# The smaller of two scores, from GpSimd to VectorE, inside a top-32 attention kernel

## The chip, the core and the metric

The kernel is one program on one NeuronCore of a Trainium2 chip. The metric is the time of one execution on the device in microseconds (us); lower is better. A core has TensorE (PE in the profile, its weight loads PEld), VectorE (DVE), ScalarE (ACT), GpSimd (POOL) and SyncE (SP, which issues transfers here).

## What is computed

The reference is attention in which each query keeps its 32 largest scores, then a mixture of eight experts, then a feed-forward layer. The change lies in the first part alone:

```python
B, H, S, D = q.shape                      # 4, 8, 576, 64
top_k = 32
scores = scale * np.matmul(q, k.transpose(0, 1, 3, 2))
kth = np.partition(scores, -top_k, axis=-1)[..., -top_k:-top_k + 1]
mask = scores >= kth
scores = np.where(mask, scores, -1000000000.0)
scores = scores - np.max(scores, axis=-1, keepdims=True)
attn = np.exp(scores)
attn = attn / (np.sum(attn, axis=-1, keepdims=True) + 1e-09)
return np.matmul(attn, v).astype(np.float32)
```

Behind it each token goes to one of 8 experts (512 to 1024 to 512) and then through 512 to 2048 to 512.

## The kernel before

**Units and groups.** The 32 heads are taken as 16 pairs (`j`). A pair has 9 units: 8 tiles of 128 queries of one head, and one tile with the last 64 queries of both heads. A unit's scores are 128 rows of 576 columns. Two units form a group `g`; there are 144 units and 72 groups, so two pairs take nine groups. The order of the work on every engine is the order in which the code is written: one loop over `g`, with background steps attached to a group by `at(g, f, ...)`.

**Scores.** For group `g + 4` TensorE multiplies q and k (both split into a high and a low part, `qh`/`ql` and `kh`/`kl`), and ScalarE copies the result to a tile of four units, `s` (L203). The parts of a pair `j` are made ahead of time: `kh` on VectorE (L170), `kl` on GpSimd (L174), `qh` on GpSimd (L178) in the same group as `kl`, `ql` on GpSimd (L182) one group later. By the loop, `kl` and `qh` of pair `j` stand in group `9j // 2 - 6`.

**Top-32 of a group.** `topk(g)` finds the 32nd largest score of each row on VectorE. A row of 576 is folded twice. `big` is the larger of columns x and x + 288; `c` (144 columns) the larger of the two halves of `big`, `lit2` the smaller of them; `lit` (288 columns) is the smaller of the two scores that `big` was made from. The 8 largest of `lit2` and of `lit` go into 16 further columns of `c`, and then four rounds of "8 largest" (L250, L261) with "replace these 8" (L258) between them are done on 160 columns instead of 576. `edge` and `top` are copied by GpSimd (L234) at the head of the next group, for a check at the end that no row needed more than the 8. `nm`, the bias for the exponential, is one small GpSimd instruction (L251) as soon as the first 8 largest are known.

**Who folds when.** `big`, `c` and `lit2` are made on VectorE for four units at once, two groups ahead: in a group with an odd number, right behind the first "8 largest" (L211 to L213). The first two groups have folds of their own. So there are 35 folds of four units and two of two. `lit` is made apart. For most groups GpSimd makes it, since the larger and the smaller of two numbers add up to their sum, bit pattern by bit pattern: as integers, `lit = a + b - big`, in `less` (L223 the sum, one group ahead, at the head of `topk`; L225 the difference, behind `nm`). In groups 0 and 1 and in the four of `DIRECT` (67, 68, 70, 71) VectorE makes it with one minimum over two units (L239).

**Behind it.** ScalarE makes the exponentials `e` (needs `nm`) and the mask `w` (needs the 32nd), TensorE transposes them, ScalarE copies `a`, TensorE multiplies by v, ScalarE copies `xr`; once per pair VectorE makes the reciprocals `r` (L335, L336), and GpSimd the scaled rows `x` (L339) and `xtail` (L344). From about 500 us on GpSimd also sends rows to memory for the experts (L837).

Of the kernel before, what the change touches and what calls it, by code (L numbers as in the profile page):

```python
# [7 lines left out]
F32 = mybir.dt.float32  # L8
F32R = mybir.dt.float32r
BF16 = mybir.dt.bfloat16  # L10
I32 = mybir.dt.int32
AF = mybir.ActivationFunctionType
ALU = mybir.AluOpType
# [3 lines left out]
B, H, S, D = 4, 8, 576, 64  # L17
# [25 lines left out]
AHEAD = 4  # L43
LEAVE = 3
START = (0, 1, 1, 2, 2, 3)
DIRECT = (67, 68, 70, 71)
FIRST = (0, 4, 9, 13)
NT1 = FIRST[B - 1]
SEG = ((0, 512), (512, S))
# [12 lines left out]
class Kernel:  # L62
# [32 lines left out]
    def attention(self, moe):  # L95
        nc, tc = self.nc, self.tc
        with ExitStack() as ctx:
            P = self.P
# [34 lines left out]
            raw, kq, st, xr = {}, {}, {}, {}  # L133
# [71 lines left out]
            def fold(s):  # L205
                h, q = S // 2, S // 4
                n = s.shape[1]
                big = P.wk.tile([128, n, h], F32, name="big", bufs=1)
                c = P.wk.tile([128, n, q + 16], F32, name="c")
                lit2 = P.wk.tile([128, n, q], F32, name="lit2", bufs=1)  # L210
                nc.vector.tensor_tensor(big, s[:, :, 0:h], s[:, :, h:S], op=ALU.max)  # L211
                nc.vector.tensor_tensor(c[:, :, 0:q], big[:, :, 0:q], big[:, :, q:h], op=ALU.max)
                nc.vector.tensor_tensor(lit2, big[:, :, 0:q], big[:, :, q:h], op=ALU.min)  # L213
                return [[t[:, i:i + 2] for t in (c, lit2, big)] for i in range(0, n, 2)]

            folded, lits, moved = {}, {}, []

            def less(g, parts):

                i = st[g].bitcast(I32)  # L220
                if parts[0]:
                    lits[g] = P.wk.tile([128, 2, S // 2], I32, name="lit")
                    nc.gpsimd.tensor_tensor(lits[g], i[:, :, 0:S // 2], i[:, :, S // 2:S], op=ALU.add)  # L223
                if parts[1]:
                    nc.gpsimd.tensor_tensor(lits[g], lits[g], folded[g][2].bitcast(I32), op=ALU.subtract)  # L225

            def topk(g):
                q = S // 4
                two = range(2)
                after_it = 2 <= g + 1 < ng and g + 1 not in DIRECT  # L230
                if after_it:
                    less(g + 1, (True, False))
                while moved:
                    nc.gpsimd.tensor_copy(*moved.pop(0))  # L234
                if g < 2:
                    folded[g], = fold(st[g])
                if g < 2 or g in DIRECT:
                    lits[g] = P.wk.tile([128, 2, S // 2], I32, name="lit")
                    nc.vector.tensor_tensor(lits[g].bitcast(F32), st[g][:, :, 0:S // 2], st[g][:, :, S // 2:S], op=ALU.min)  # L239
                c, lit2, _ = folded.pop(g)  # L240
                lit = lits.pop(g).bitcast(F32)
                m8 = P.wk.tile([128, 2, TOPK // 8, 8], F32, name="m8", bufs=4)
                z = P.wk.tile([128, 2, q + 16], F32, name="z", bufs=1)
                nm = P.wk.tile([128, 2], F32, name="nm", bufs=4)
                for i in two:
                    nc.vector.max(c[:, i, q + 8:q + 16], lit2[:, i])
                for i in two:
                    nc.vector.max(c[:, i, q:q + 8], lit[:, i])
                for i in two:
                    nc.vector.max(m8[:, i, 0], c[:, i])  # L250
                nc.gpsimd.tensor_scalar(nm, m8[:, :, 0, 0], -0.125, None, op0=ALU.mult)  # L251
                if g % 2 and g + 1 < ng:
                    folded[g + 1], folded[g + 2] = fold(four[g // 2 + 1])
                if after_it:
                    less(g + 1, (False, True))
                for r in range(TOPK // 8 - 1):
                    for i in two:
                        nc.vector.match_replace(out=z[:, i], in_to_replace=m8[:, i, r],  # L258
                                                in_values=c[:, i] if r == 0 else z[:, i], imm_value=LOWEST)
                    for i in two:  # L260
                        nc.vector.max(m8[:, i, r + 1], z[:, i])  # L261
                last = m8[:, :, TOPK // 8 - 1, 7:8]
                moved.append((edge[:, 2 * g:2 * g + 2], c[:, :, q + 7::8]))
                moved.append((top[:, 2 * g:2 * g + 2], last[:, :, 0]))
                return [(last[:, i], nm[:, i:i + 1]) for i in two]
# [88 lines left out]
            ng = nu // 2  # L354
# [25 lines left out]
            for j in range(1, len(pairs)):  # L380
                g = 9 * j // 2 - AHEAD - 4
# [109 lines left out]
            for g in range(ng):  # L491
                for f, a in first.pop(g, []):
                    f(*a)
                tk[g] = topk(g)
                if g > 0:
                    ws = masks(g - 1)
# [1171 lines left out]
```

## Time and profile before

| what | us |
|---|---|
| median of 3 runs | 1267.04 (1265.31 to 1267.12) |
| the profiled execution's own time | 1264.6 |
| its span, first to last instruction | 1263.0 |
| busy in the span: TensorE, VectorE, ScalarE, GpSimd | 1141.2, 925.2, 739.1, 676.8 |
| last "8 largest" of the last group ends | about 535 |
| the feed-forward layer, on TensorE, begins | about 833 |

Busy time is the union of an engine's instructions in the profile. It contains waits that happen inside an instruction: a record that is longer than another of the same operation and shape has waited for something after it was issued. A table row of the trace's list in order of time gives the start, the duration and, where an engine sat idle, for how long and what released it; consecutive instructions of an engine may overlap by some 0.08 us.

### The profile page before, as it was taken

The numbers are of one execution on the slowest core, as the hardware profiler recorded it, in microseconds if no ns is written. First come the engines' busy times: TensorE is split into PE (matmuls) and PEld (weight loads), VectorE is DVE, ScalarE is ACT, GpSimd is POOL, SyncE is SP. The second block draws the span as 40 slices with busy tenths as digits, with TensorE's granted clock in tenths as the row PEclk, the third lists the DMA queues.
The fourth block names the chain that finished last, engine by engine and source line by source line (L and its number), as shares of the span: only waits on it lengthen the run. The fifth ranks groups of instructions, "written<-read, shape, count | busy, mean of one in ns | idle before, by whom it ended". The sixth has DMA issues, their size and how long they took to land. (4 is left out here: it accounts for less than half of the span.)

```text
span 1263.0 us, 25811 instructions
## 1 busy us (share of the span) xinstructions
PE 1141.2 (90%) x9220; PEld 972.8 (77%) x9221; DVE 925.2 (73%) x2573; ACT 739.1 (59%) x1328; POOL 676.8 (54%) x724
## 2 busy tenths in 40 slices
PE   8988899889989997787987898988899999999998
PEld 5766677668767776576776797877799999999997
DVE  6999999999999999986999995658722232222222
ACT  4878787789778886734665666643433333333322
POOL 3877787778777775762666552315532322223221
PEclk7999999989988998998989999999999999999999
DMA  4126463102020102356777777733110101000000
GB/s 90 26 89 203 146 212 116 44 11 49 11 49 11 30 11 86 127 177 199 255 240 242 240 253 240 231 122 109 36 42 9 34 17 34 18 25 26 25 1 25
DMA packets 139219, 123.56 MB, mean 98 GB/s; under 512 B 65408, under 2 KB 102272, under 8 KB 139072
## 3 DMA queue, kind: packets, MB, share of 16 engines
q1 hardware_dynamic: 133312, 108.05, 27.8%
q0 software_dynamic: 3392, 11.27, 2.7%
q10 hardware_dynamic: 2368, 2.39, 0.6%
q8 instruction: 78, 1.28, 0.4%
q14 instruction: 69, 0.57, 0.1%
HBM read 87.07 MB, written 34.60 MB: 96 GB/s over the span
## 5 line engine op out<-in xcount | busy, mean ns | idle before, releaser
L1166 POOL TENSOR_TENSOR gl<-g,gh 128x384 fp32r<-128x384 f32 x96 | 98.4, 1025 | 285.2 <-ACT gh L1165 246.7
L297 PE MATMUL tp<-nhuge,w 128*128 128x128 bf16 x720 | 143.4, 233 | 41.4 <-ACT w L286 41.4
L1327 POOL TENSOR_TENSOR w1l<-w1r,w1h 128x512 fp32r<-128x512 f32 x72 | 103.0, 1433 | 131.9 <-ACT w1h L1326 90.9
L295 PE MATMUL tp<-ident,e 128*128 128x128 f32 x720 | 157.6, 306 | 8.0 <-ACT e L281 8.0
L1161 ACT ACTIVATE c<-c,half 128x384 f32<-128x384 f32 x96 | 59.2, 617 | 178.7 <-DVE c L1160 178.6
L1160 DVE TENSOR_SCALAR c<-h 128x384 f32<-128x384 f32 x95 | 52.7, 555 | 145.4 <-PE h L1019 145.4
L295 PEld LDWEIGHTS tp<-ident,e 128*128 128x128 f32 x720 | 109.7, 152 | 38.4 <-ACT e L281 10.7
L1016 PE MATMUL h<-xh,wih 128*128 128x384 f32 x380 | 129.1, 340 | 1.1 <-ACT xh L1010 1.1
L1017 PE MATMUL h<-xh,wil 128*128 128x384 f32 x380 | 128.8, 339 | 0.0
L286 ACT ACTIVATE w<-s,m 128x576 bf16<-128x576 f32 x144 | 103.5, 769 | 36.9 <-DVE m L261 36.9
L281 ACT ACTIVATE e<-s,nm 128x576 f32<-128x576 f32 x144 | 103.4, 767 | 33.4 <-POOL nm L251 33.2
L1163 DVE TENSOR_TENSOR g<-c,h 128x384 f32<-128x384 f32 x95 | 52.6, 554 | 95.0 <-ACT c L1161 95.0
L1027 PE MATMUL y<-woh,gl 128*128 128x512 f32 x288 | 114.9, 399 | 4.7 <-POOL gl L1166 4.7
L297 PEld LDWEIGHTS <-w 128*128 128x128 bf16 x720 | 81.6, 114 | 48.0 <-ACT w L286 47.7
L261 DVE MAX8 m<-z 128x8 f32<-128x160 f32 x432 | 116.6, 309 | 0.0
L1025 PE MATMUL y<-woh,gh 128*128 128x512 f32 x288 | 112.8, 392 | 3.4 <-ACT gh L1165 3.4
L302 ACT ACTIVATE a<-tp 128x640 f32<-128x640 f32 x144 | 101.6, 706 | 22.4 <-PE tp L297 20.4
L1026 PE MATMUL y<-wol,gh 128*128 128x512 f32 x288 | 113.6, 395 | 0.0
L225 POOL TENSOR_TENSOR lit<-lit,big 128x576 int32<-128x576 int32 x66 | 103.0, 1561 | 1.5 <-POOL nm L251 0.4
L1327 DVE TENSOR_TENSOR w2l<-w2r,w2h 128x512 fp32r<-128x512 f32 x86 | 88.1, 1028 | 20.5 <-ACT w2h L1326 19.8
L314 PE MATMUL tp<-v,a 128*64 128x65 f32 x2880 | 102.4, 226 | 0.3 <-ACT a L302 0.2
L223 POOL TENSOR_TENSOR lit<-s 128x576 int32<-128x576 int32 x66 | 101.9, 1545 | 1.1
(309 smaller groups left out, 3254.8 us busy)
## 6 DMA issues: line engine op xcount, KB each, us to landing
w1r<-in_moe_w_dram SPq DMA_DIRECT2D x88, 256.0 KB, 3.7
w2r<-in_moe_w_dram SPq DMA_DIRECT2D x88, 256.0 KB, 3.6
xs_dr<-zero SPq DMA_DIRECT2D x19, 512.0 KB, 4.7
ys_dr<-zero SPq DMA_DIRECT2D x19, 512.0 KB, 5.4
cr<-in_moe_w_in_dram SPq DMA_DIRECT2D x16, 512.0 KB, 4.5
cr<-in_moe_w_out_dram SPq DMA_DIRECT2D x13, 512.0 KB, 3.6
rows<-xs_dr SPq DMA_DIRECT2D x20, 256.0 KB, 2.8
rk<-in_k_dram SPq DMA_DIRECT2D x32, 128.0 KB, 2.6
```

Of the source, the lines that this page charges most:

```text
L225: nc.gpsimd.tensor_tensor(lits[g], lits[g], folded[g][2].bitcast(I32), op=ALU.subtract)
L261: nc.vector.max(m8[:, i, r + 1], z[:, i])
L281: nc.scalar.activation(e, s, AF.Exp, bias=nm, scale=0.125)
L286: nc.scalar.activation(w, s, AF.Relu, bias=t, scale=-1.0)
L295: nc.tensor.matmul(o, e[:, k0:k0 + 128], self.ident, is_transpose=True, start=True, stop=False)
L297: nc.tensor.matmul(o, w[:, k0:k0 + 128], self.nhuge, start=False, stop=True)
L1016: nc.tensor.matmul(p, wh[c], xh[:, c, :], start=c == 0, stop=False)
L1017: nc.tensor.matmul(p, wl[c], xh[:, c, :], start=False, stop=False)
L1025: nc.tensor.matmul(y[t], hh[:, o], wh, start=first, stop=False)
L1026: nc.tensor.matmul(y[t], hh[:, o], wl, start=False, stop=False)
L1027: nc.tensor.matmul(y[t], hl[:, o], wh, start=False, stop=last)
L1327: sub(l, w, h.bitcast(F32), op=ALU.subtract)
```

## The change

The minimum `lit` moves into `fold`, on VectorE, for four units at once and right behind `lit2`. `less`, `DIRECT` and GpSimd's two integer operations per group are gone. The four later groups that VectorE served apart, and the first two, now take `lit` from their fold too.

```diff
-DIRECT = (67, 68, 70, 71)
...
                 lit2 = P.wk.tile([128, n, q], F32, name="lit2", bufs=1)
+                lit = P.wk.tile([128, n, h], F32, name="lit", bufs=1)
                 nc.vector.tensor_tensor(big, s[:, :, 0:h], s[:, :, h:S], op=ALU.max)
                 nc.vector.tensor_tensor(c[:, :, 0:q], big[:, :, 0:q], big[:, :, q:h], op=ALU.max)
                 nc.vector.tensor_tensor(lit2, big[:, :, 0:q], big[:, :, q:h], op=ALU.min)
-                return [[t[:, i:i + 2] for t in (c, lit2, big)] for i in range(0, n, 2)]
-
-            folded, lits, moved = {}, {}, []
-
-            def less(g, parts):
-
-                i = st[g].bitcast(I32)
-                if parts[0]:
-                    lits[g] = P.wk.tile([128, 2, S // 2], I32, name="lit")
-                    nc.gpsimd.tensor_tensor(lits[g], i[:, :, 0:S // 2], i[:, :, S // 2:S], op=ALU.add)
-                if parts[1]:
-                    nc.gpsimd.tensor_tensor(lits[g], lits[g], folded[g][2].bitcast(I32), op=ALU.subtract)
+                nc.vector.tensor_tensor(lit, s[:, :, 0:h], s[:, :, h:S], op=ALU.min)
+                return [[t[:, i:i + 2] for t in (c, lit2, lit)] for i in range(0, n, 2)]
+
+            folded, moved = {}, []
 
             def topk(g):
                 q = S // 4
                 two = range(2)
-                after_it = 2 <= g + 1 < ng and g + 1 not in DIRECT
-                if after_it:
-                    less(g + 1, (True, False))
                 while moved:
                     nc.gpsimd.tensor_copy(*moved.pop(0))
                 if g < 2:
                     folded[g], = fold(st[g])
-                if g < 2 or g in DIRECT:
-                    lits[g] = P.wk.tile([128, 2, S // 2], I32, name="lit")
-                    nc.vector.tensor_tensor(lits[g].bitcast(F32), st[g][:, :, 0:S // 2], st[g][:, :, S // 2:S], op=ALU.min)
-                c, lit2, _ = folded.pop(g)
-                lit = lits.pop(g).bitcast(F32)
+                c, lit2, lit = folded.pop(g)
...
                 if g % 2 and g + 1 < ng:
                     folded[g + 1], folded[g + 2] = fold(four[g // 2 + 1])
-                if after_it:
-                    less(g + 1, (False, True))
```

Line numbers after L213 differ between the two programs: `kl`, `qh`, `ql` are L174, L178, L182 before and L173, L177, L181 after, `nm` is L251 and L236, the copies `edge` and `top` are L234 and L223, the "8 largest" L246, L248, L250, L261 are L231, L233, L235, L244.

GpSimd's queue in groups 3 and 4, before: from the `nm` of group 3 to the `nm` of group 4 and its `ql`.

```order
L251 TENSOR_SCALAR nm<-m_572 128x2
L225 TENSOR_TENSOR lit<-lit,big 128x576
L174 TENSOR_TENSOR kl<-kT,kh 128x576
L178 TENSOR_TENSOR qh_115<-qT,zero 128x512
L223 TENSOR_TENSOR lit<-s 128x576
L234 COPY edge<-c 128x4
L234 COPY top<-m_572 128x2
L251 TENSOR_SCALAR nm<-m_680 128x2
L225 TENSOR_TENSOR lit<-lit,big 128x576
L182 TENSOR_TENSOR ql_116<-qT,qh_115 128x512
```

The same stretch after:

```order
L236 TENSOR_SCALAR nm<-m_566 128x2
L173 TENSOR_TENSOR kl<-kT,kh 128x576
L177 TENSOR_TENSOR qh_115<-qT,zero 128x512
L223 COPY edge<-c 128x4
L223 COPY top<-m_566 128x2
L236 TENSOR_SCALAR nm<-m_673 128x2
L181 TENSOR_TENSOR ql_116<-qT,qh_115 128x512
```

`kl` and `qh` now stand right behind `nm`, as does `ql` one group on.

GpSimd's queue from the `x` of group 16 to the `ql` of group 17, before.

```order
L339 TENSOR_TENSOR x_73<-xr,r 128x4x128
L344 TENSOR_TENSOR xtail_77<-xr,r 64x64 x2
L223 TENSOR_TENSOR lit<-s_1903 128x576
L234 COPY edge<-c 128x4
L234 COPY top<-m_2097 128x2
L251 TENSOR_SCALAR nm<-m_2208 128x2
L225 TENSOR_TENSOR lit<-lit,big 128x576
L182 TENSOR_TENSOR ql_118<-qT,qh_117 128x512
```

The same stretch after:

```order
L322 TENSOR_TENSOR x_73<-xr,r 128x4x128
L327 TENSOR_TENSOR xtail_77<-xr,r 64x64 x2
L223 COPY edge<-c 128x4
L223 COPY top<-m_2066 128x2
L236 TENSOR_SCALAR nm<-m_2174 128x2
L181 TENSOR_TENSOR ql_118<-qT,qh_117 128x512
```

Only the three short instructions are left between `xtail` and `ql`.

VectorE's queue at the fold in group 3, before (`m` is the tile of the 32 largest, `lit_584` is `lit2`).

```order
L250 MAX m_572<-c 128x8 x2
L211 TENSOR_TENSOR big<-s 128x1152
L212 TENSOR_TENSOR c<-big 128x4x144
L213 TENSOR_TENSOR lit_584<-big 128x576
L258 MATCH_REPLACE z<-m_572,c 128x160 x2
```

The same place after (`lit_578` is `lit2`):

```order
L235 MAX m_566<-c 128x8 x2
L211 TENSOR_TENSOR big<-s 128x1152
L212 TENSOR_TENSOR c<-big 128x4x144
L213 TENSOR_TENSOR lit_578<-big 128x576
L214 TENSOR_TENSOR lit<-s 128x1152
L241 MATCH_REPLACE z<-m_566,c 128x160 x2
```

One instruction, the minimum of 1152 columns, has come between `lit2` and the first match.

## Rows read from the trace of the kernel before

**Rows 1.** The page, part 1: busy us (share of the span) and instructions.

```profile
PE 1141.2 (90%) x9220; PEld 972.8 (77%) x9221; DVE 925.2 (73%) x2573; ACT 739.1 (59%) x1328; POOL 676.8 (54%) x724
```

**Rows 2.** Busy us by stretch: length, engines with instructions, granted clock, DMA share, GB/s.

```profile
40.00:535.00 495.00, 432.17 (x5355) 354.62 (x5352) 491.33 (x1861) 395.77 (x696) 379.44 (x464) 0.95 0.25 76
```

**Rows 3.** Groups on GpSimd, 40 to 480 us: count, busy us, mean ns, idle before.

```profile
L225 POOL TENSOR_TENSOR lit<-lit,big 128x576 int32<-128x576 int32 x62 | 96.8, 1562 | 1.4 <-POOL nm L251 0.4
```

**Rows 4.** VectorE in order of time, fold of group 3: start us, duration us.

```profile
43.28 1.33 DVE L211 TENSOR_TENSOR big<-s 128x1152 f32<-128x1152 f32 x1
44.65 0.76 DVE L212 TENSOR_TENSOR c<-big 128x576 f32<-128x576 f32 x1
45.32 1.98 DVE L213 TENSOR_TENSOR lit<-big 128x576 f32<-128x576 f32 x1
47.23 0.08 DVE L258 MATCH_VALUE_LOAD z<-m,c 128x8 f32 x1
```

**Rows 5.** GpSimd in order of time, the same fold.

```profile
43.45 1.24 POOL L251 TENSOR_SCALAR nm<-m 128x2 f32<-128x2 f32 x1 [1.65 <-DVE m L250]
44.76 1.92 POOL L225 TENSOR_TENSOR lit<-lit,big 128x576 int32<-128x576 int32 x1
46.65 1.94 POOL L174 TENSOR_TENSOR kl<-kT,kh 128x576 fp32r<-128x576 f32 x1
```

**Rows 6.** VectorE in order of time, fold of group 69 and around it.

```profile
515.18 0.82 DVE L248 MAX8 c<-lit 128x8 f32<-128x288 f32 x2 [0.55 <-POOL lit L225]
...
516.37 1.34 DVE L211 TENSOR_TENSOR big<-s 128x1152 f32<-128x1152 f32 x1
...
519.09 0.08 DVE L258 MATCH_VALUE_LOAD z<-m,c 128x8 f32 x1
...
522.77 1.60 DVE L239 TENSOR_TENSOR lit<-s 128x576 f32<-128x576 f32 x1
```

**Rows 7.** VectorE in order of time, the fold that group 1 makes for itself.

```profile
23.20 1.54 DVE L212 TENSOR_TENSOR c<-big 128x288 f32<-128x288 f32 x1
24.66 1.51 DVE L213 TENSOR_TENSOR lit<-big 128x288 f32<-128x288 f32 x1
26.10 1.82 DVE L239 TENSOR_TENSOR lit<-s 128x576 f32<-128x576 f32 x1
```

**Rows 8.** GpSimd in order of time, the same fold.

```profile
22.58 1.84 POOL L174 TENSOR_TENSOR kl<-kT,kh 128x576 fp32r<-128x576 f32 x1 [5.00 <-DVE kh L170]
24.39 1.47 POOL L178 TENSOR_TENSOR qh<-qT,zero 128x512 fp32r<-128x512 f32 x1
25.94 1.36 POOL L182 TENSOR_TENSOR ql<-qT,qh 128x512 fp32r<-128x512 f32 x1
```

**Rows 9.** Line L239: duration ns least/median/most, first and last start.

```profile
L239 DVE TENSOR_TENSOR lit<-s x6: 737/752/1820, 14.9 to 529.3; 128x576 f32<-128x576 f32 x6
```

**Rows 10.** GpSimd in order of time, ahead of the fold of group 17.

```profile
141.82 1.88 POOL L344 TENSOR_TENSOR xtail<-xr,r 64x64 f32<-64x64 f32 x2
```

**Rows 11.** VectorE in order of time, fold of group 23.

```profile
182.97 2.00 DVE L211 TENSOR_TENSOR big<-s 128x1152 f32<-128x1152 f32 x1
...
185.69 3.50 DVE L213 TENSOR_TENSOR lit<-big 128x576 f32<-128x576 f32 x1
```

**Rows 12.** GpSimd in order of time, the same fold.

```profile
185.80 1.40 POOL L225 TENSOR_TENSOR lit<-lit,big 128x576 int32<-128x576 int32 x1
187.16 1.41 POOL L223 TENSOR_TENSOR lit<-s 128x576 int32<-128x576 int32 x1
```

**Rows 13.** VectorE in order of time, fold of group 9.

```profile
88.44 0.75 DVE L213 TENSOR_TENSOR lit<-big 128x576 f32<-128x576 f32 x1
```

**Rows 14.** GpSimd in order of time, the same fold.

```profile
88.56 1.91 POOL L225 TENSOR_TENSOR lit<-lit,big 128x576 int32<-128x576 int32 x1
```

**Rows 15.** VectorE in order of time, fold of group 13.

```profile
114.10 1.71 DVE L212 TENSOR_TENSOR c<-big 128x576 f32<-128x576 f32 x1
```

**Rows 16.** Line L335: duration ns least/median/most, first and last start.

```profile
L335 DVE TENSOR_SCALAR r<-xr x20: 96/160/1287, 78.5 to 543.1; 128x9 f32<-128x9 f32 x15, 128x2 f32<-128x2 f32 x4, 128x1 f32<-128x1 f32 x1
```

## The prediction

> **What bounds the kernel now.** I read the page's busy line first: over the whole span no engine but TensorE is above 73% [rows 1]. That average mixes stages, so I took the busy time by stretches next. From 40 to 535 us VectorE works 491.3 of 495 us, TensorE 432, ScalarE 396 and GpSimd 379 [rows 2]. So up to the last top-32 (about 534 us) the time is the length of VectorE's queue, and what a change adds to that queue or takes from it moves everything behind it by as much. GpSimd's part of the job (L225 and its twin L223, two integer operations per group) takes 1.56 us apiece and 96.8 us for the 62 instances of L225 between 40 and 480 us [rows 3]. It is large, but GpSimd is not the bound.
>
> Then I looked inside a fold, because its durations don't fit its sizes. In the fold at 43.28 us, `big` (1152 columns) takes 1.33 us and `c` (576) 0.76, but `lit2`, of the same size as `c`, takes 1.98; from the start of `big` to the first match it is 3.95 us [rows 4]. GpSimd shows why: its L225 was issued 0.11 us into `c`, took 1.92 us, and `lit2` ends only after it; the next GpSimd operation, a `kl`, then lasts 1.94 because `lit2` was in front of it [rows 5]. Two-input operations of the two engines exclude each other, and they alternate. Of the 35 four-unit folds 27 last 3.93 to 4.01 us like this one. At 516.37 us, where GpSimd has no such work, the same three operations need 2.72 us [rows 6] (one other fold, at 502.82, is like it). So GpSimd's two operations are not free to VectorE: they cost it about 1.2 us per fold.
>
> **The change, part by part.** *Added:* one minimum over 1152 columns per four-unit fold, 35 of them. Its nearest row is `big`, of the same shape: 1.33 us, of which some 0.08 overlaps the next instruction (as `lit2` and the match do in [rows 4]), so 1.25. A fold that GpSimd leaves alone becomes 2.72 + 1.25 = 3.97 us. Against today's 3.95 that is nothing: the relief of `lit2` pays for the new operation almost exactly. The result hangs on the folds that are not left alone.
>
> *Moved:* with L223 and L225 gone, GpSimd's remaining two-input work (`kl` and `qh`, then `ql` one group later, for each head pair) moves forward to right behind `nm`, as the rows of order show. `nm` is released just before the fold; so in a group with odd number this work now meets the fold, where before it came later and met the matches, which don't mind. By the loop, `kl`+`qh` come in an odd group for pairs 2, 3, 6, 7, 10, 11, 14, 15 (eight folds) and `ql` for six others. That they alternate with VectorE, one for one, the fold at 22.42 us shows, the only one where GpSimd has a run of such work today: `c` and `lit2`, of 288 columns and so shorter than the 0.76 us of [rows 4], take 1.54 and 1.51, and the 576 columns of `lit` 1.82 where its like take 0.75 (the middle of L239 [rows 9]), each behind one of `kl`, `qh`, `ql` [rows 7, 8]. So:
> - `kl`+`qh` in a fold: `lit2` waits for `kl` (1.21: 1.97 as today behind L225, less 0.76), `lit` for `qh` (1.07: 1.82 less 0.75): 3.97 + 2.28 = 6.25 us, against 3.95 today.
> - `ql` in a fold: 3.97 + 1.07 = 5.05.
> - In six of these fourteen (groups 17, 21, 35, 39, 53, 57) `x` and `xtail` of the group before come first. Today the second `xtail` is caught by `big` there: the pair takes 1.88 us from 141.82, with the `big` of that fold inside [rows 10]. Behind it now stand `edge`, `top` and `nm`, short ones, and then `ql` or `kl`+`qh`. Who goes first then is a race that the trace shows both ways. At 182.97 `lit2` lost to L225 and L223, one after the other, and took 3.50 us [rows 11, 12]; at 88.44, with L225 issued 0.12 us after it instead of 0.11, it took 0.75 and L225 waited [rows 13, 14]. Four folds went the second way, three the first. Won, the short ones cost the fold some 0.2 us: 4.2. Lost, `lit2` waits for them (0.4 us) and for `ql` as well (1.3 [rows 8]): 3.97 + 1.7 = 5.7; with `kl`+`qh`, of which the second comes before `lit2` or before `lit`, 1.25 more: 6.95. These are estimates from those rows.
>
> The sum over the 35 folds. Today: 27 x 3.95, three at 4.91 (a late `qh` makes `c` 1.71 us long [rows 15]), three at 6.15 [rows 11], two at 2.72 or a little more = 145.3 us. After: 21 alone x 3.97 = 83.4; five with `kl`+`qh` x 6.25 = 31.3; three with `ql` x 5.05 = 15.2; the six doubtful ones 25.2 if all are won, 38.0 if all are lost, 31.6 with half of each, which I take, since the trace has four to three. Total 161.5 (155.1 to 167.9), so +16.2 (+9.8 to +22.6).
>
> *Removed from VectorE:* the four separate minima of groups 67, 68, 70, 71 (L239), three at 0.67 (0.75 less the overlap) and the one at 522.77, behind an `x`, at 1.53 [rows 6, 9]: -3.5. The `r` of three groups, which stood up to 1.29 us instead of the middle 0.16 behind a late `qh` [rows 16]: -3.4. The wait of 0.55 us for the last L225, before the max at 515.18 [rows 6]: -0.5. Sum of these -7.4. In groups 0 and 1 the same minimum merely changes its line: nothing.
>
> *Costed at nothing:* GpSimd's lost 200 us, hidden already under a full VectorE; the new tile `lit`, as large as the two it replaces, read and written by VectorE alone; the longer fold's effect on `w` and `e` on ScalarE and on the copies behind it, which are late with VectorE and not in addition to it. What is queued behind a delayed `lit` is the match loop of the group, and with it all that I count. After 535 us no instruction changes, and I let the shift pass through unaltered.
>
> **Net: +16.2 - 7.4 = +8.8 us** (+2.4 to +15.2 from the race alone). The profiled execution took 1264.6 us, so 1273.4; the median of the three runs is 1267.04, which gives 1275.8. I say 1275.
>
> [...] The row to explain is `lit2` at 185.69 us, issued ahead of L225 (185.80) and L223 (187.16) and still behind both [rows 11, 12]. [...]
>
> **The rivals.**
> 1. *VectorE wins all six races.* For it: the four folds like 88.44 us; against: the three like 182.97. Time: +2.4, so 1267.0 by the profiled execution or 1269.4 by the median, at the edge of what can be told from no change. Chance 0.2.
> 2. *The other side: the shared access is simply relieved.* If `kl`, `qh` and `ql` came too late to be queued before `lit2` (`kl` must be issued within 0.63 us of `nm`'s end, which is when `lit2` is), all 35 folds would last 3.97: 139 us, -6.3, with the -7.4 in all -13.7, so 1251 to 1253. It decides when fewer than six of the `kl`+`qh` folds collide, since each costs 2.28. Against it: L225 came 0.07 us after `nm` in [rows 5] and `kl` has nothing else to wait for, its `kh` being ready before the group starts. Chance 0.09.
> 3. *No relief.* If `nm` and the small copies block the fold as L225 does, the new minimum comes on top: 35 x 1.25 - 7.4 = +36, 1301. Against it: in [rows 4, 5] `nm` waits for `big` and ends 0.04 us into `c`, and `c` still takes its 0.76. Chance 0.03.
>
> My own case, with some of the races lost (+5 to +15), has 0.62; 0.06 is left for small mishaps either way.
>
> **How the numbers follow.** This kernel's measurement tells about 0.2% (2.5 us) from no change. Slower by more: my case, rival 3, and the upper half of rival 1: 0.73. Within: the rest of rival 1 and small mishaps: 0.16. Faster: rival 2 and a little: 0.11. The range runs from 1266, just below rival 1, to 1283, all races lost on top of the median; it leaves out rivals 2 and 3.
>
> **What would show it.** Right: the fold's four operations at 1.33, 0.76, 0.76 and 1.33 us in most groups; `lit2` near 1.97 and `lit` near 2.4 in groups 3, 7, 25, 43, 61; `lit2` at 1.8 in 13, 31, 49; `r` never above 0.2 us before 500 us; VectorE still full to about 543 us. Wrong: idle time on VectorE before that, folds of 3.97 in groups 3 and 7 (then rival 2), small copies that hold up `c` (rival 3), or a stretch after 535 us that changes its length.

## The result, and the profile after

The changed kernel took 1278.97 us (median of 4 runs, 1276.64 to 1279.64) against 1267.08 (1265.31 to 1268.04): a ratio of 1.0092, 95% interval 1.0075 to 1.011. A second set on another occasion gave 1276.01 against 1267.34, 1.0069 (1.0045 to 1.0093). So the change made the kernel 9 to 12 us slower. The profiled execution took 1279.38 us.

First the page and the busy time by stretch, which answer to [rows 1, 2].

```profile
PE 1161.2 (91%) x9220; PEld 989.4 (77%) x9221; DVE 923.9 (72%) x2604; ACT 738.9 (58%) x1328; POOL 484.0 (38%) x592
```

```profile
40.00:535.00 495.00, 438.03 (x5195) 360.44 (x5194) 486.84 (x1859) 383.81 (x673) 188.25 (x328) 0.89 0.25 75
```

GpSimd has lost 193 us of work and VectorE, with 31 more instructions, is busy as long as before: the relief has paid for the new minima. But between 40 and 535 us VectorE is now idle for 8.2 us (3.7 before), and TensorE's granted clock is 0.89 there (0.95 before, third number from the end).

The fold of group 17, VectorE and then GpSimd in order of time. It is one of the six that the prediction called doubtful.

```profile
146.75 1.34 DVE L211 TENSOR_TENSOR big<-s 128x1152 f32<-128x1152 f32 x1
148.20 0.76 DVE L212 TENSOR_TENSOR c<-big 128x576 f32<-128x576 f32 x1
148.87 0.75 DVE L213 TENSOR_TENSOR lit<-big 128x576 f32<-128x576 f32 x1
149.54 1.35 DVE L214 TENSOR_TENSOR lit<-s 128x1152 f32<-128x1152 f32 x1
150.81 0.08 DVE L241 MATCH_VALUE_LOAD z<-m,c 128x8 f32 x1
```

```profile
148.31 0.70 POOL L223 COPY edge<-c 128x4 f32<-128x4 f32 x1
148.95 0.72 POOL L223 COPY top<-m 128x2 f32<-128x2 f32 x1
149.64 1.33 POOL L236 TENSOR_SCALAR nm<-m 128x2 f32<-128x2 f32 x1
150.93 1.27 POOL L181 TENSOR_TENSOR ql<-qT,qh 128x512 fp32r<-128x512 f32 x1
```

VectorE loses nothing: from `big` to the first match it is 4.06 us, as in 26 of the 35 folds (eight others meet GpSimd's long operations, and in group 15 `c` starts 0.46 us late, as a row at run 7 shows). The short instructions, 0.19, 0.19 and 0.22 us by the medians of their lines, stretch to 0.70, 0.72 and 1.33: each waits out one VectorE operation, and so `ql` is issued when the fold is over.

The fold of group 3, with `kl` and `qh` behind `nm`, VectorE and then GpSimd; it answers to [rows 4, 5].

```profile
43.36 1.35 DVE L211 TENSOR_TENSOR big<-s 128x1152 f32<-128x1152 f32 x1
44.81 1.95 DVE L212 TENSOR_TENSOR c<-big 128x576 f32<-128x576 f32 x1
46.68 1.84 DVE L213 TENSOR_TENSOR lit<-big 128x576 f32<-128x576 f32 x1
48.45 1.35 DVE L214 TENSOR_TENSOR lit<-s 128x1152 f32<-128x1152 f32 x1
49.71 0.08 DVE L241 MATCH_VALUE_LOAD z<-m,c 128x8 f32 x1
```

```profile
43.53 1.25 POOL L236 TENSOR_SCALAR nm<-m 128x2 f32<-128x2 f32 x1 [1.64 <-DVE m L235]
44.74 1.41 POOL L173 TENSOR_TENSOR kl<-kT,kh 128x576 fp32r<-128x576 f32 x1
46.10 1.80 POOL L177 TENSOR_TENSOR qh<-qT,zero 128x512 fp32r<-128x512 f32 x1
```

Two collisions, 6.36 us in all, as forecast (6.25), but one instruction earlier: `c` and `lit2` wait, not `lit2` and `lit`, because `c` starts 1.45 us behind `big` instead of 1.37 and `kl` is issued 0.07 us ahead of it. In groups 13, 31 and 49 `ql` meets `c` in the same way (1.82 us) and not `lit2`.

In sum the 35 folds take 157.1 us, +11.8 over 145.3. Yet the last of the 32-largest maxima ends at 543.3 us instead of 534.7, and what follows it is 6.2 us longer (734.4 against 728.2 us to the end of the span). The end of the last maximum, before and then after:

```profile
534.20 0.55 DVE L261 MAX8 m<-z 128x8 f32<-128x160 f32 x2
542.78 0.54 DVE L244 MAX8 m<-z 128x8 f32<-128x160 f32 x2
```

The folds can't have made all of the 8.6 us, since 3.5 and 3.4 us are taken off VectorE elsewhere (the four separate minima and the long `r`), and they have no part in the 6.2. The `r` of VectorE in order of time shows where to look; the bracket is the idle time before it and what ended it.

```profile
530.49 0.17 DVE L318 TENSOR_SCALAR r<-xr 128x9 f32<-128x9 f32 x1 [2.88 <-ACT xr L311]
...
538.24 0.17 DVE L318 TENSOR_SCALAR r<-xr 128x2 f32<-128x2 f32 x1 [2.39 <-ACT xr L308]
...
550.71 0.17 DVE L318 TENSOR_SCALAR r<-xr 128x2 f32<-128x2 f32 x1 [4.87 <-POOL top L520]
```

`xr` is the end of a group's way through ScalarE and TensorE. The two waits before 543 us, 5.3 us, have no counterpart before the change, where the first such wait comes behind the last maximum:

```profile
536.58 0.17 DVE L335 TENSOR_SCALAR r<-xr 128x2 f32<-128x2 f32 x1 [1.24 <-ACT xr L325]
```

The stretches of the changed kernel around them (length, busy us of PE, PEld, DVE, ACT, POOL, then the granted clock):

```profile
492.00:495.00 3.00, 0.44 (x2) 0.14 (x1) 3.00 (x19) 1.98 (x3) 0.36 (x2) 1.00 0.00 0
501.00:504.00 3.00, 0.67 (x7) 0.47 (x9) 3.00 (x19) 2.64 (x6) 2.05 (x4) 0.84 0.60 195
504.00:514.00 10.00, 9.98 (x76) 8.14 (x74) 9.79 (x37) 5.25 (x10) 8.76 (x15) 0.50 0.58 206
514.00:524.00 10.00, 6.46 (x59) 4.87 (x59) 9.90 (x35) 2.55 (x6) 7.53 (x16) 0.50 0.48 185
524.00:534.00 10.00, 10.00 (x80) 8.20 (x78) 7.03 (x38) 4.27 (x9) 3.33 (x13) 0.51 0.44 133
```

TensorE stood nearly idle twice around VectorE's routing sums (495.2 to 499.2 us): its list shows a wait of 2.57 us for a mask `w` that ends at 495.99, and one of 2.45 us, put down to GpSimd's sending of rows, that ends at 503.33. Its granted clock fell to 0.50 at 496.2 us for 3.4 us and again at 503.0, and this time it stayed there for 30.7 us. At that clock it is full from 504 to 514 and from 524 to 534 us, and from 524 us on it is VectorE that has gaps (7.03 us busy of 10). One of the products with v takes 0.32 us in the mean from 504 to 514 us, and 0.22 at 1.00 from 502 to 512 us before the change. In the kernel before, a similar place looks like this:

```profile
492.00:502.00 10.00, 7.55 (x68) 6.19 (x67) 9.59 (x49) 6.37 (x12) 4.35 (x8) 0.68 0.46 145
502.00:512.00 10.00, 8.54 (x106) 7.44 (x106) 9.90 (x38) 6.84 (x12) 8.73 (x19) 1.00 0.52 200
512.00:522.00 10.00, 7.92 (x116) 5.56 (x115) 9.41 (x39) 5.87 (x12) 8.14 (x15) 1.00 0.28 107
```

The clock dips there too, twice for 3.4 us, but it is back at 502 us. The last product with v of the attention, on TensorE, before and then after:

```profile
539.33 1.39 PE L314 MATMUL tp<-v,a 128*64 128x65 f32 x40
553.46 1.39 PE L297 MATMUL tp<-v,a 128*64 128x65 f32 x40
```

It ends 6.0 us behind the last maximum before the change and 11.5 us behind it after: 5.5 of the 6.2 us are there already.

### The profile page after: what moved, and what is told of

It is laid out like the page before. It is cut to its first block, busy times and chain, and to the rows that moved or that the text cites. A ratio compares the mean times of both kernels' runs of the same rounds, so it can differ in the third digit from the quotient of the medians.

```text
span 1277.7 us, 25768 instructions
## 1 busy us (share of the span) xinstructions
PE 1161.2 (91%) x9220; PEld 989.4 (77%) x9221; DVE 923.9 (72%) x2604; ACT 738.9 (58%) x1328; POOL 484.0 (38%) x592
## 5 line engine op out<-in xcount | busy, mean ns | idle before, releaser
L280 PE MATMUL tp<-nhuge,w 128*128 128x128 bf16 x720 | 146.7, 236 | 47.5 <-ACT w L269 46.2
L278 PE MATMUL tp<-ident,e 128*128 128x128 f32 x720 | 160.4, 311 | 5.5 <-ACT e L264 3.0
L278 PEld LDWEIGHTS tp<-ident,e 128*128 128x128 f32 x720 | 111.7, 155 | 38.1 <-issue 11.2
L244 DVE MAX8 m<-z 128x8 f32<-128x160 f32 x432 | 117.3, 313 | 0.0
L297 PE MATMUL tp<-v,a 128*64 128x65 f32 x2880 | 107.8, 233 | 0.1
L297 PEld LDWEIGHTS tp<-v,a 128*64 128x64 f32 x2880 | 97.2, 146 | 13.5 <-ACT a L285 4.8
L202 ACT ACTIVATE s<-sp 128x576 f32<-128x576 f32 x144 | 92.6, 644 | 17.6 <-PE sp L194 12.3
```

Source lines behind the costliest of these rows:

```text
L278: nc.tensor.matmul(o, e[:, k0:k0 + 128], self.ident, is_transpose=True, start=True, stop=False)
L280: nc.tensor.matmul(o, w[:, k0:k0 + 128], self.nhuge, start=False, stop=True)
L297: nc.tensor.matmul(o[HS[i]], a[:, k0:k0 + 64], v_[:, u % 2 if u < 8 else i, kc, :], start=kc == 0, stop=kc == 4)
```

## The experiments

The theory after the result has two parts: the folds make VectorE's queue a little longer, by access taken in turns, and with the new timing there is a stretch in which TensorE stays at its lower clock (0.50), which makes the rest of the loss. Against it: the minimum's own cost or its relief is different from what the folds seem to say, or the clock is a bystander.

**1. The cost without the relief.** The kernel before, with the minimum added and GpSimd's operations kept:

```diff
                 nc.vector.tensor_tensor(lit2, big[:, :, 0:q], big[:, :, q:h], op=ALU.min)
+                if n == 4:
+                    more = P.wk.tile([128, n, h], F32, name="more", bufs=1)
+                    nc.vector.tensor_tensor(more, s[:, :, 0:h], s[:, :, h:S], op=ALU.min)
```

> The kernel before with one more minimum over 1152 columns behind lit2 in each of the 35 four-unit folds, into a tile that nobody reads; GpSimd's two integer operations stay. It is the change's cost without its relief. Theory of exclusive access, taken in turns: each fold gets 1.27 us for the minimum (what it took by start to start in the changed kernel) and, in the some 30 folds where a further GpSimd operation is queued behind L225, about 1.2 us more, because that one now goes before the new minimum: +65 to +85 us over the kernel before. Rival, the minimum costs its own length alone: +44 us. Rival, it hides: 0.

1332.22 us (1328.96 to 1336.38), against 1267.00: +65 us, ratio 1.0523 (1.0475 to 1.0571). The 35 folds take 208.9 us, +63.6, and the last top-32 ends 63.0 us later. Its fold of group 3, VectorE and then GpSimd:

```profile
47.08 0.76 DVE L212 TENSOR_TENSOR c<-big 128x576 f32<-128x576 f32 x1
47.75 1.96 DVE L213 TENSOR_TENSOR lit<-big 128x576 f32<-128x576 f32 x1
49.64 2.57 DVE L216 TENSOR_TENSOR more<-s 128x1152 f32<-128x1152 f32 x1
```

```profile
47.19 1.90 POOL L228 TENSOR_TENSOR lit<-lit,big 128x576 int32<-128x576 int32 x1
49.06 1.93 POOL L174 TENSOR_TENSOR kl<-kT,kh 128x576 fp32r<-128x576 f32 x1
50.96 2.40 POOL L178 TENSOR_TENSOR qh<-qT,zero 128x512 fp32r<-128x512 f32 x1
```

The new minimum of 1.35 us takes 2.57: `kl`, itself held up by `lit2`, goes before it. So the engines do take turns, and the minimum is neither hidden nor worth its own length alone. The result lies at the lower end of the forecast because in 19 of the 35 folds no long GpSimd operation comes up for that last turn and the minimum takes 1.35 to 1.38; in the other 16, and not in some 30, it takes about 2.57.

**2. The relief without the cost.** The changed kernel without the minima; `lit` is a constant tile, `low`, filled once with a very low number, so the smaller score of each of a row's 288 pairs is left out:

```diff
-                lit = P.wk.tile([128, n, h], F32, name="lit", bufs=1)
+                lit = low[:, 0:n] if n == 4 else P.wk.tile([128, n, h], F32, name="lit", bufs=1)
...
-                nc.vector.tensor_tensor(lit, s[:, :, 0:h], s[:, :, h:S], op=ALU.min)
+                if n < 4:
+                    nc.vector.tensor_tensor(lit, s[:, :, 0:h], s[:, :, h:S], op=ALU.min)
```

> The changed kernel without the 35 minima of four units: lit is a constant tile of very low numbers, so the 32 largest are taken without that quarter of the candidates. It is the change's relief without its cost. Theory (VectorE's queue is the time up to the last top-32): 35 x 1.27 = 44 us less than the changed kernel, some 32 us less than the kernel before. Rival, TensorE or ScalarE ends the stage once VectorE is relieved: less than 30 us below the changed kernel, with idle time on VectorE between 40 and 480 us.

1224.50 us (2 runs), 42.5 below the kernel before on that chip (0.9662, 0.9609 to 0.9715). The folds take 112.3 us, 44.8 below the changed kernel's 157.1, as expected, and the list of waits shows none of VectorE between 40 and 493 us, where the last top-32 ends:

```profile
40.00:490.00 450.00, 417.27 (x5308) 347.37 (x5307) 444.94 (x1832) 390.18 (x688) 179.72 (x329) 0.96 0.27 83
```

So VectorE's queue is the time of this stage, and no other engine holds it up even when VectorE has 45 us less to do. The whole is 54 us below the changed kernel's first set, 10 more than the folds: in its trace no `r` waits for `xr` before the last top-32, as it did there (5.3 us), and what follows the last top-32 is 4.3 us shorter.

**3. GpSimd's work out of the folds' way.** The changed kernel with other groups for `kl`, `qh` and `ql`:

```diff
+                odd = g % 2
...
-                at(g + 2, krest, j, *eng)
-                at(g + 2, qparts, j)
-                at(g + 3, qrest, j, *eng)
+                at(g + 2 + odd, krest, j, *eng)
+                at(g + 2 + odd, qparts, j)
+                at(g + 2 if j and j % 4 == 0 else g + 3, qrest, j, *eng)
```

> The changed kernel with kl and qh moved from odd groups to the next (even) group, and ql of every fourth pair one group earlier, so that GpSimd's two-input work no longer meets a fold; nothing else differs. Theory (the collisions cost 2.30 us in five folds and 1.07 in three): 14.7 us less than the changed kernel, so about 1264, at or just below the kernel before, and all 35 folds at 4.06 us. Rival, the folds only swap one wait for another, or the late parts hold up TensorE: no change from the changed kernel, 1277 to 1280.

1252.41 us (1250.01 to 1254.24), 0.9879 (0.9834 to 0.9923) of the kernel before. The folds take 143.0 us, 14.1 below the changed kernel: the price of the collisions was right, and GpSimd's work costs VectorE's queue nothing to speak of where it meets matches and maxima (the last top-32 ends 19.8 us earlier: 14.1 from the folds, 5.3 from the waits of `r`). Its fold of group 3, VectorE:

```profile
43.04 1.35 DVE L211 TENSOR_TENSOR big<-s 128x1152 f32<-128x1152 f32 x1
44.49 0.76 DVE L212 TENSOR_TENSOR c<-big 128x576 f32<-128x576 f32 x1
45.16 0.75 DVE L213 TENSOR_TENSOR lit<-big 128x576 f32<-128x576 f32 x1
45.83 1.35 DVE L214 TENSOR_TENSOR lit<-s 128x1152 f32<-128x1152 f32 x1
47.10 0.08 DVE L241 MATCH_VALUE_LOAD z<-m,c 128x8 f32 x1
```

But the time fell by 26 us, 12 more than the forecast. The two waits of `r` are gone, and what follows the last top-32 is 6.4 us shorter. This trace too has a stretch at 0.50, 17 us from 480, and no `r` waits before the last top-32, so a low stretch doesn't by itself make VectorE wait.

**4. TensorE kept at work.** The changed kernel with spare matmuls:

```diff
                 if g + 3 >= ng:
                     self.warm(P.misc(), 4)
+                elif g + 7 >= ng:
+                    self.warm(P.misc(), 8)
```

> The changed kernel with 8 spare matmuls of 512 columns into an unread bank in each of groups 65 to 68, where TensorE sits idle while VectorE does the routing; its granted clock there fell to 0.50 from 503 to 534 us in the changed kernel. Theory (part of the loss is TensorE at its lower clock, which makes r wait for xr on VectorE): the clock stays up, the waits of r at 527 to 550 us go, 5 to 9 us less than the changed kernel, 1270 to 1274. Rival, the clock is a bystander and VectorE's queue alone made the loss: no change, 1277 to 1280.

1266.61 us (10 runs, 1263.74 to 1271.48), 0.9998 (0.9976 to 1.0021) of the kernel before. Added work made the kernel 12 us faster than the changed kernel in its first set and 9 faster than in its second, where 5 to 9 were expected. The folds are the same to 0.1 us (157.1); the clock by stretch is not:

```profile
501.00:511.00 10.00, 7.93 (x56) 5.21 (x57) 9.79 (x36) 4.95 (x9) 8.43 (x13) 0.50 0.69 237
511.00:521.00 10.00, 10.00 (x115) 8.41 (x113) 10.00 (x48) 6.73 (x12) 8.38 (x19) 0.99 0.41 159
521.00:531.00 10.00, 9.04 (x133) 6.90 (x132) 9.81 (x42) 8.46 (x17) 6.47 (x15) 1.00 0.58 187
```

It falls as well, which was not expected, but is back after 10 us instead of 31. `r` no longer waits before the last top-32, which ends at 537.7 us, 3.0 later than before the change instead of 8.6.

**5. The same matmuls in the kernel before.**

> The kernel before with the same 8 spare matmuls in each of groups 65 to 68 as the changed kernel got in the run called a_warm. It separates the two causes: what the change costs when TensorE's clock is no part of it is a_warm (1266.6) less this. Theory (VectorE's queue got 3 to 4 us longer, by the end of the last top-32 at 537.7 against 534.7 us): this one gains a little too, from the two low stretches of 3.4 us at 491 and 498 us, 1262 to 1265. Rival, the kernel before has nothing to win there: 1267, and the change by itself is worth nothing either way.

1263.02 us (12 runs, 1259.97 to 1267.62), 0.997 (0.9955 to 0.9986). So the kernel before gains 0.3% too, and the change without the long low stretch is worth the difference between 0.9998 and 0.997: some 0.3%, or 3.6 us slower. These are two sets, each against its own runs of the kernel before, and the difference is hardly larger than its uncertainty; the end of the last top-32 is the firmer measure and says the same (537.7 against 534.5, +3.2). Why the kernel before gains isn't shown: its last top-32 ends only 0.2 us earlier, and the rest of the gain lies behind it.

**6. Both edits together**, 3 and 4.

> The changed kernel with kl, qh and ql out of the folds' way (as in a_even) and the spare matmuls in groups 65 to 68 (as in a_warm). Theory (two separate causes): 14 us below a_warm, so 1250 to 1253, and no more than 3 us below a_even, whose last low stretch of 17 us at 480 made nothing wait before the last top-32. Rival, a_even's 26 us below the changed kernel were the moved work alone: the spare matmuls then only cost, 1253 to 1256.

1252.09 us (1251.25 to 1255.33), 0.9883 (0.9859 to 0.9907): 14.5 below run 4, as the folds alone give (142.9 us), and no different from run 3. So the two causes add up, but the moved work removes both: run 3 had got rid of the waits without the spare matmuls.

**7. A third buffer for `c`**, first alone and then on top of 6:

```diff
-                c = P.wk.tile([128, n, q + 16], F32, name="c")
+                c = P.wk.tile([128, n, q + 16], F32, name="c", bufs=3)
```

> The changed kernel with a third buffer for c and nothing else. In the changed kernel c starts 1.45 us after big and kl gets in front of c instead of lit2. Theory (the late start is a wait on GpSimd's copy out of c): c starts 0.07 to 0.08 us earlier in the undisturbed folds, the 35 folds are 2 to 3 us shorter in sum, about 154.5 us; the folds with kl and qh stay near 6.3. The time follows only if the long stretch of low clock stays as it is: 1276 with it, 1264 without. Rival: the folds stay at 157.1 in sum.

1275.59 us (1272.60 to 1276.88), 1.0065 (1.0042 to 1.0087), no different from the changed kernel beside it (1276.01). The folds take 154.7 us, 2.4 less. Its fold of group 7, VectorE:

```profile
73.73 1.34 DVE L211 TENSOR_TENSOR big<-s 128x1152 f32<-128x1152 f32 x1
75.10 0.76 DVE L212 TENSOR_TENSOR c<-big 128x576 f32<-128x576 f32 x1
75.78 1.97 DVE L213 TENSOR_TENSOR lit<-big 128x576 f32<-128x576 f32 x1
77.67 2.41 DVE L214 TENSOR_TENSOR lit<-s 128x1152 f32<-128x1152 f32 x1
80.01 0.08 DVE L241 MATCH_VALUE_LOAD z<-m,c 128x8 f32 x1
```

`c` starts at 1.37 again, and `kl` and `qh` meet `lit2` and `lit`, at the 1.97 and 2.4 us that the prediction gave. That holds for four of the five folds with `kl` and `qh`; in group 3 `c` still starts 0.07 us late and meets `kl`. So the 0.08 us is the wait of `c` for GpSimd's copy, and it decides which two operations collide, at nearly the same price (6.29 against 6.36 us). In group 15 of the changed kernel the same wait is long enough for the list to name it, and with the third buffer it is gone:

```profile
134.06 0.76 DVE L212 TENSOR_TENSOR c<-big 128x576 f32<-128x576 f32 x1 [0.46 <-POOL edge L223]
```

The clock was low in two stretches of 10 and 14 us here, and `r` waited 2.97 and 1.00 us before the last top-32.

> As a_even_warm, with a third buffer for c, so that c need not wait for GpSimd's copy out of the buffer before last. In the changed kernel c starts 1.45 us after big, 0.08 later than in the kernel before (1.37), and carries a wait on GpSimd there. Theory (that wait is the 0.08): folds of 3.98 instead of 4.06 us, 35 x 0.08 = 2.8 us below a_even_warm. Rival, the gap has another cause: folds stay at 4.06 and the time with them.

1250.67 us (1248.80 to 1252.48), 0.987 (0.9847 to 0.9893): the fastest version, 15 us below the kernel before. That the third buffer adds to run 6 is seen in the folds alone (140.5 against 142.9 us); the intervals overlap.

**8. The changed kernel again.**

> The changed kernel once more, unaltered, beside the kernel before on one chip. Question: is TensorE's long stretch at a granted clock of 0.50 (503 to 534 us in the changed kernel's trace) a property of this program or an accident of one execution. Theory (the order of the work brings it about): it is there again, with r waiting for xr before the last top-32 ends near 543 us, and the time is 8 to 14 us over the kernel before. Rival (accident): no such stretch, the last top-32 ends near 538 us, and the time is 2 to 5 us over the kernel before.

1276.01 us (4 runs, 1274.91 to 1276.43). The long stretch is there again, 30.7 us from 502.1, and `r` waits 2.90 and 2.00 us for `xr`. So it is no accident of one execution but belongs to this program's timing. The last product with v ends 11.5 us behind the last maximum here too, but at the end of the program only 2.3 of the 5.5 us are left.

## Why the prediction was right, and where not

The forecast was 1275 with a range of 1266 to 1283; the measured time lies in it, on the forecast side. But the sum came out by two errors that cancel, and that they do is luck: VectorE's own queue grew by some 3.3 us instead of 8.8, and TensorE, on which the sum has no term, made up the difference and more. Two of the prediction's own signs of being wrong are in the trace: idle time on VectorE before 543 us, and a longer stretch behind the last top-32.

**What held.** *VectorE's queue sets the time of the stage*: shown by runs 1 and 2, where +63.6 and -44.8 us in the folds moved the end of the last top-32 by as much, but for the waits of `r`. *The relief pays for the minimum*: an undisturbed fold went from 3.95 to 4.06 us (forecast 3.97; the 0.08 more is the wait of `c`, run 7). *`kl`+`qh` in five folds at 6.25 and `ql` in three at 5.05*: 6.36 and 5.12. That these are the collisions and nothing else, run 3 showed. *What is removed, -7.4*: `r` never takes more than 0.2 us before 550 us, and neither the four separate minima nor the wait for L225 are left. From start to start the minima give 3.51 us and the `r` 3.36, as forecast; the waits for L225 were 1.66 us over eight groups and not 0.5 in one, so that 8.5 us went in all.

**The step that failed first: "the six doubtful ones ... 31.6 with half of each, which I take".** None was lost; all six take 4.06 us, 24.4 together. With them the folds came to 157.1 and not 161.5, +11.8 and not +16.2. The prediction took the three lost folds of the kernel before [rows 11, 12] as a sample of a race. In the changed kernel three short instructions stand between `xtail` and `ql` (or `kl`), and each of them waits for a whole VectorE operation (0.70, 0.72 and 1.33 us in group 17), so the long one behind them is not issued inside any of the six folds (`ql` at 150.93 us, the fold of group 17 over at 150.81). At 182.97 us in the kernel before, the same three stood ahead of L225, but `edge` was issued 0.66 us into `big`, a whole operation earlier, and L225 came up at `lit2`, so that fold was no pattern for these six. That none is lost is what rival 1 said. In the fold of group 17 `edge` was issued 0.11 us behind `c` and ends 0.05 us behind it (149.01 and 148.96 us). VectorE's queue by itself became 3.0 us longer (run 4) to 3.3 (the end of the last top-32 less the two waits, and also 11.8 less 8.5), where the prediction said 8.8 and its rival 1 2.4. Why L225 and L223 both passed `lit2` at 185.69 us in the kernel before stays open.

**The step that failed second: "After 535 us no instruction changes, and I let the shift pass through unaltered"**, and with it the silence on TensorE. In the changed kernel the stage was no longer VectorE's alone once TensorE stayed at its lower clock (0.50 from 503.0 to 533.7 us). The two profiled executions are 14.8 us apart by their spans: 5.3 are the waits of `r` before the last top-32, 6.2 came behind it, 5.5 of them where TensorE was late with the last groups, and 3.3 are VectorE's own. Of the 6.2 not all is sure: what follows the last top-32 took 723.8 to 734.4 us in the traces of the whole computation, and 723.8 and 728.2 in two with the same folds as the kernel before. Run 4 took back 9 to 12 us by keeping TensorE at work and changing no fold. That the low clock makes the waits is shown by that run and by the rows of TensorE full at 0.50 (9.98 and 10.00 us busy of 10). What lets the clock stay down for 31 us in the changed kernel, and only for 3.4 us twice at that place in the kernel before, is not settled: both have idle stretches of TensorE ahead of it (busy 0.71 and 1.20 us of 3 before, from 489 and from 495 us; 0.44 and 0.67 of 3 after, from 492 and from 501).

**The rivals.** Relief alone, -13.7, would have needed folds without collisions; the change did not bring them about, but run 3 did, and came out 14.6 us below the kernel before (11.2 by the end of the last top-32). No relief, +36, is refuted by run 2, whose folds are 33 us shorter than those of the kernel before.

## What to carry to other kernels

When two engines exclude each other, as `c` and `kl` do in group 3 (1.95 us instead of 0.76), moving an operation from one to the other changes two things: its own length, and what stands next in the other engine's queue at the same moment. Here the first came to nothing and the second decided the folds, so the gain (15 us) lay in moving the remaining work of the other engine to where it meets instructions that don't mind (in the changed kernel a match of 160 columns takes 0.30 to 0.32 us throughout and a maximum over as many 0.30 to 0.33). Before you let a shift pass through to the end of a program, look at the engine that is second in the stage, and for TensorE at the granted clock behind every stretch in which it idles: here it read 0.50 for 30.7 us behind a stretch with 0.67 us of work in 3, and 32 spare matmuls were worth 9 to 12 us, as much as the change had cost.

## What the runs showed that I had not expected

- In six folds short GpSimd instructions seem to have protected VectorE: `edge`, `top` and `nm`, 0.19, 0.19 and 0.22 us by the medians, waited out one VectorE operation apiece (0.70, 0.72, 1.33 us), and the long `ql` or `kl` behind them came after the fold. No run takes them away, so that they are what protected it is read from the rows alone.
- A wait that costs 0.08 us (`c` on GpSimd's copy) decided in four folds which operations collide: `c` and `lit2` (1.95, 1.84 us) or `lit2` and `lit` (1.97, 2.41).
- TensorE's granted clock stayed at 0.50 from 504 to 514 us although TensorE was busy 9.98 of 10 us. It had fallen at 503.0 us, in a stretch with 0.67 us of work in 3 (from 501). In run 4, with the spare matmuls, it fell too, but for 10 us, and the time was 9 to 12 us lower.
